# Large SBUF tiles handed out first in a fixed sequence, each beginning on a whole 128-byte line

## The chip, the cores and the metric

The kernel runs on one core of one Trainium2 chip. The metric is device time in microseconds of that core, the median of several runs. The core has five engines that run side by side: TensorE (PE, matrix products; its weight loads are listed as PEld), VectorE (DVE), ScalarE (ACT), GpSimd (POOL) and SyncE (SP), which here only issues DMA transfers. SBUF, the memory that the engines work in, has 128 partitions; a tile takes the same bytes in each of them, so that its place is one address within a partition.

## The reference

Two kinds of layer alternate, four in all, on a 2048 x 512 activation in float32. Layer A is a two-dimensional Fourier filter, layer B a gated bilinear feed-forward block with 1792 hidden features.

```python
def _A_ref(x, w_r, w_i):
    B, S, D = x.shape
    X = jnp.fft.rfft2(x, axes=(-2, -1))
    X = X * (w_r + 1j * w_i)
    return jnp.fft.irfft2(X, s=(S, D), axes=(-2, -1))

def _B_ref(x, w_gate, w_up, w_down):
    g = jnp.einsum("bsd,df->bsf", x, w_gate)
    u = jnp.einsum("bsd,df->bsf", x, w_up)
    return jnp.einsum("bsf,fd->bsd", g * u, w_down)

x = A_x
x = x + _A_ref(_layernorm(x), A_w_r, A_w_i)
x = x + _B_ref(_layernorm(x), B_w_gate, B_w_up, B_w_down)
x = x + _A_ref(_layernorm(x), A_w_r, A_w_i)
x = x + _B_ref(_layernorm(x), B_w_gate, B_w_up, B_w_down)
```

## The kernel before

**What it computes, and how.** The activation stays in SBUF throughout, as the tile `xs` of 16 blocks of 128 x 512. A Fourier layer is a chain of small float32 products (`fwd` with the tile `tp`, `middle` with `dp`, `zp` and `vq`, `inv` with `yi` and `yo`). A feed-forward layer splits every float32 factor into a high and a low part in the type float32r and takes three products in place of one: high by high, high by low, low by high (`mm3`). It also saves products of blocks by sums and differences of the blocks (the forms of the input in the tiles `xA` and `xS`, those of the weights in `wt`). One call of `prod` in `unit` is six matmuls of one weight form (stationary, a slice of 128 columns of `wt`) with one input form (moving, 512 or 256 columns of `xA` or `xS`); a call of `unit` is seven such products, named `gw, gx, gy, gx, gz, gv, gz` after the PSUM tile that they write. The way down again takes one of two paths: in the first half of the first layer, and at the very end of the second, `db` products (stationary the hidden block `h`, moving the weights `wd`, 512 columns); elsewhere `down`, with forms of hidden blocks as stationary operand (`sf`, or a part of a `bf` tile) and forms of the down weights as moving one (`bf`, 256 columns), into `ex, ey, ew, ez, ev`.

**What sets the order.** Every operation is recorded in `Plan` and then put out in the sequence that the table `ORDER` holds; a second table, `PLACES`, says which buffer of its ring a tile gets. The engines keep this order. Nothing in it is decided from addresses.

**What sets the addresses.** The three pools of SBUF and PSUM hand out addresses one after the other. A buffer is known by its tag (ring and number, such as `xA0` or `f3`) and gets its place when a tile of that tag is first asked for, that is when the first operation that uses it is put out (`Tile_.__call__` calls `make`, which calls `wk.tile`). Every buffer is rounded up to 32 bytes. The pool `cp` comes first and ends at byte 52,128 of a partition with the tile `hp`; the pool `wk`, with all other tiles of SBUF, begins there. So the offsets of the buffers of `wk` within a line of 128 bytes come from what small buffers (`st`, `mv`, `rs`: 32 bytes each) happened to be asked for before them. The built program has these places (bytes; in brackets the remainder by 128):

```text
buffer                             before            after
xs, midt, ident (pool cp)     16512.. [0]       the same
xA0: forms of the input       101792 [32]        52224 [0]
xS0: forms of the input        64928 [32]        76800 [0]
wa0, wa1, wb0, wb1: wt   196064, 202208,   109568, 123904,
                   218592, 210400 [96]   115712, 130048 [0]
rg0: slots of sf, raw weights  97696 [32]       138240 [0]
sx0: slots of sf, u            224736 [96]      142336 [0]
e0: E, xf, hw                  150784 [0]       146432 [0]
h0: bf, h, tws                  54176 [32]      179200 [0]
wd0: bf, wd, a part of wq      132000 [32]      187392 [0]
f0 to f10 (11 buffers of 2 KB)    all four       all four
dc, dj, tw (df, di, twiddles)         [32]            [0]
```

Whatever slice of 128 columns of a large tile a matmul takes, it lies a multiple of 512 bytes from the tile's beginning and so has the tile's remainder.

In this document two operands of a matmul have **equal offsets** when stationary and moving operand begin at the same remainder. Before, `db` products have equal offsets (`wd` and `h` at 32; both parts of `hw`, at the end, at 0). Products with `wt` do not (96 and 32). Products with `bf` do when the stationary operand is in `rg0` or in a `bf` tile (1,044 of 1,680 matmuls), and do not when it is in `sx0` (636).

All instructions of the plan carry the line of the helper that records them (L307 in the profile), so that the rows below are told apart by their tiles.

Of the kernel before, what the change touches and what calls it, by code (L numbers as in the profile page):

```python
# [11 lines left out]
F32 = mybir.dt.float32  # L12
# [90 lines left out]
SWAPS = "2212212212212212", "2212212212212212"  # L103
FAST = (0, 1)
IDLE = 2, 3
FAHEAD, BOFF, COFF, IOFF, W1, HPDUE, TOFF = 2.79, 9.0, 6.0, 5.0, 10.0, 40.0, 6.0
UFIRST = 5.0
UNITS = ((7.5, 17.4, 15.0), (7.2, 16.9, 16.9)), ((7.2, 16.9, 14.5), (7.2, 14.5, 14.5))
# [168 lines left out]
def kernel(ctx: ExitStack, tc: tile.TileContext, x, wf, wc, wb, dfwd, tf, ti, mid, out):  # L277
    nc = tc.nc
    cp = ctx.enter_context(tc.tile_pool(name="cp", bufs=1))
    wk = ctx.enter_context(tc.tile_pool(name="wk", bufs=1))  # L280
    pp = ctx.enter_context(tc.tile_pool(name="pp", bufs=1, space=bass.MemoryType.PSUM))
    dr = ctx.enter_context(tc.tile_pool(name="dr", bufs=1, space=bass.MemoryType.DRAM))
    plan = Plan()
# [49 lines left out]
    def load(kb, fn, r, w, **kw):  # L333
        return plan.op("SP", 0.1, 2.5, fn, r, w, kb=kb, **kw)
# [49 lines left out]
    def load_di():  # L384
        t = temp("di", "dj", (128, 4, 256))
        load(512, lambda: SP.dma_start(t(), dfwd[:, 512:1536].rearrange("p (b n) -> p b n", b=4)), (), [t])
        return t
# [123 lines left out]
    def keep_warm(n):  # L511
        for i in range(n):
            bk = bank("wp", "w")
            pe(0.86, lambda bk=bk: TE.matmul(bk(), midt[:, 0:128], midt, start=True, stop=True), ["midt"], [bk, "idle"])
# [462 lines left out]
    for layer in range(2):  # L977
        dcs["i"] = load_di()
        keep_warm(IDLE[layer])
        for g in range(16):  # L980
# [22 lines left out]
        t = t1  # L1003
# [21 lines left out]
        for k, (ft, half, h0) in enumerate(seq):  # L1025
# [32 lines left out]
            else:  # L1058
                first = ft // 2 not in blocks or (half is not None and (ft // 2, half) not in begun)
# [24 lines left out]
        else:  # L1084
            for t in range(8, 16):
                load(256, lambda t=t: SP.dma_start(out[:, t], xs[:, t]), [("xs", t)], [("out", t)], due=t0)
    for o in plan.order():
        o["fn"]()


# [42 lines left out]
```

## Time and profile before

| | us |
|---|---|
| median of 3 runs | 1082.05 (1081.18 to 1082.25) |
| the profiled execution | 1080.65 |
| its span, first to last instruction | 1078.9 |
| PE busy in it | 1054.7 |
| DVE, POOL, ACT busy | 817.1, 752.2, 406.5 |

What lies around the span is 1080.65 - 1078.9 = 1.75 us. The granted TensorE clock is 0.999 of full speed over the span.

How to read the rows: a row of a timeline gives the start of a run of instructions, the time from the start of the first to the end of the last, the tiles out<-in, the partitions by columns of the stationary operand, the shape of the output, and their number. Matmuls are pipelined: the next one starts long before the last has ended, so the pace is read from the starts of rows that follow each other, not from the duration of one. Six matmuls to a row is one product.

### The profile page before, as it was taken

To read this page: it belongs to the slowest core of one execution; us is meant where nothing else is said; L and a number is where in the kernel's file an instruction comes from. 1 tells how busy PE (TensorE), PEld (TensorE's weight loads), DVE (VectorE), ACT (ScalarE), POOL (GpSimd) and SP (SyncE) were. 2 spreads that over 40 slices of the span, in tenths; PEclk is the share of its full clock that TensorE was granted. 3 is DMA by queue.
4 is the path that set the end of the run, shared out by engine and by line. 5 is a ranking of instruction groups with operands and counts; after the bars stand their busy time and mean duration, and the time that the engine had idled before them with its cause. 6 is when DMAs were issued, how large, how long until landed. Compare 5 with 4: busy or idle time off the path is not lost.

```text
span 1078.9 us, 18673 instructions
## 1 busy us (share of the span) xinstructions
PE 1054.7 (98%) x6546; PEld 900.9 (84%) x6546; DVE 817.1 (76%) x1603; ACT 406.5 (38%) x965; POOL 752.2 (70%) x1000
## 2 busy tenths in 40 slices
PE   8999999999999999999989999999999999999998
PEld 6677888887899888889967779888788998888897
DVE  7677876668877567777897688688788876677688
ACT  6458534344344223223254484222323431222321
POOL 6847698989999666677747037455678994666772
PEclk9999999999999999999999999999999999999999
DMA  9514356778754765556390004465777255565542
GB/s 357 231 39 179 106 176 217 228 253 281 231 179 159 263 208 165 193 168 212 114 370 4 1 16 139 165 212 160 242 216 230 80 177 204 205 205 176 195 147 79
DMA packets 84668, 193.65 MB, mean 179 GB/s; under 512 B 39264, under 2 KB 50784, under 8 KB 73568
## 3 DMA queue, kind: packets, MB, share of 16 engines
q0 software_dynamic: 16128, 102.77, 28.8%
q1 hardware_dynamic: 68160, 89.18, 24.5%
q8 instruction: 52, 0.85, 0.3%
q10 hardware_dynamic: 288, 0.52, 0.1%
q14 instruction: 40, 0.33, 0.1%
HBM read 145.52 MB, written 46.92 MB: 178 GB/s over the span
## 4 chain that ended last, share of the span: by engine, by line
PE 80%; POOL 6%; DVE 5%; DMA 2%; issue 2%; ACT 2%; SPq 0%; DVEq 0%; POOLq 0%; ACTq 0%
PE gx L307 13%; PE gz L307 12%; PE gw L307 6%; PE gy L307 6%; PE gv L307 6%; PE db L307 5%; PE ex L307 5%; PE ez L307 4%; PE dp L307 3%; PE yi L307 3%; PE zp L307 3%; PE ev L307 2%; PE ew L307 2%; PE ey L307 2%; PE vq L307 2%; PE yo L307 2%
## 5 line engine op out<-in xcount | busy, mean ns | idle before, releaser
L307 PE MATMUL gx<-xA,wt 128*128 128x512 f32 (+1 forms) x852 | 181.5, 348 | 2.3 <-ACT s L307 2.3
L307 PEld LDWEIGHTS gx<-xA,wt 128*128 128x128 f32 x852 | 136.0, 188 | 21.9 <-ACT s L307 2.5
L307 DVE TENSOR_TENSOR xs<-xs,db 128x512 f32<-128x512 f32 x128 | 85.1, 679 | 21.6 <-PE db L307 21.2
L307 POOL TENSOR_TENSOR sf<-cc,sf 128x256 fp32r<-128x256 f32 x103 | 75.9, 740 | 24.7 <-ACT sf L307 24.3
L307 PE MATMUL gz<-xS,wt 128*128 128x512 f32 (+1 forms) x426 | 91.5, 350 | 1.1 <-DVE q L307 1.1
L307 PE MATMUL db<-wd,h 128*128 128x512 f32 x336 | 91.8, 397 | 0.0
L307 PE MATMUL gw<-xS,wt 128*128 128x512 f32 (+1 forms) x426 | 90.9, 348 | 0.3 <-POOL xS L307 0.2
L307 PE MATMUL gy<-xS,wt 128*128 128x512 f32 (+1 forms) x426 | 91.0, 349 | 0.0
L307 PE MATMUL gz<-xA,wt 128*128 128x512 f32 (+1 forms) x426 | 90.7, 348 | 0.0
L307 PE MATMUL gv<-xS,wt 128*128 128x512 f32 (+1 forms) x426 | 90.3, 347 | 0.0
L307 POOL TENSOR_TENSOR sf<-q,sf 128x256 fp32r<-128x256 f32 x89 | 65.6, 739 | 32.4 <-ACT sf L307 31.8
L307 PEld LDWEIGHTS gz<-xS,wt 128*128 128x128 f32 x426 | 68.6, 188 | 12.8 <-DVE q L307 1.7
L307 PEld LDWEIGHTS gw<-xS,wt 128*128 128x128 f32 x426 | 68.9, 188 | 11.5 <-POOL xS L307 0.7
L307 DVE TENSOR_TENSOR q<-gy,s 128x512 f32<-128x512 f32 (+1 forms) x71 | 40.9, 577 | 49.1 <-PE gy L307 26.5
L307 PEld LDWEIGHTS gy<-xS,wt 128*128 128x128 f32 x426 | 68.3, 188 | 10.4 <-issue 0.5
L307 PEld LDWEIGHTS gv<-xS,wt 128*128 128x128 f32 x426 | 68.2, 188 | 10.2 <-issue 0.7
L307 PEld LDWEIGHTS gz<-xA,wt 128*128 128x128 f32 x426 | 68.3, 188 | 10.1 <-issue 0.5
L307 ACT COPY s<-gx 128x512 f32<-128x512 f32 (+1 forms) x71 | 35.2, 496 | 105.0 <-PE gx L307 94.6
L307 POOL TENSOR_TENSOR wt<-rg,wt 128x512 fp32r<-128x512 f32 (+1 forms) x56 | 64.1, 1155 | 12.4 <-ACT wt L307 12.4
L307 PEld LDWEIGHTS db<-wd,h 128*128 128x128 f32 x336 | 61.0, 188 | 13.3 <-issue 1.2
L307 ACT CAST sf<-q 128x256 fp32r<-128x256 f32 x89 | 36.2, 406 | 87.2 <-DVE q L307 35.5
L307 POOL DMA_DIRECT2D wt<-gu x72 | 40.5, 563 | 35.5 <-PE gw L307 22.4
(163 smaller groups left out, 2551.3 us busy)
## 6 DMA issues: line engine op xcount, KB each, us to landing
wt<-gu POOLq DMA_DIRECT2D x36, 1024.0 KB, 5.3
wt<-gu POOLq DMA_DIRECT2D x36, 768.0 KB, 5.0
bf<-dn POOLq DMA_DIRECT2D x20, 1024.0 KB, 5.5
wq<-in_wf_dram SPq DMA_DIRECT2D x16, 1024.0 KB, 12.7
bf<-dn POOLq DMA_DIRECT2D x20, 768.0 KB, 4.7
gu<-wt SPq DMA_DIRECT2D x14, 1024.0 KB, 6.3
gu<-wt SPq DMA_DIRECT2D x14, 768.0 KB, 5.8
rg<-in_wb_dram SPq DMA_DIRECT2D x14, 512.0 KB, 4.3
```

What stands on the lines that cost most here:

```text
L307: ins = f(*args, **kw)
```

## The change

The change puts a table `PLACED` ahead of the placing of all buffers. It looks up the first tile of each tag in the order of the plan, then asks for these tiles in the table's sequence; an entry that is a number asks for a buffer of so many bytes per partition that nothing uses. The gap of 96 bytes takes the beginning of the pool from 52,128 to 52,224, a multiple of 128, and the sizes of the large tiles are all multiples of 128. After them the plan is put out as before, and the rest of the buffers get their places behind the large ones, in the order in which they are first used.

```diff
+PLACED = (96, 'xA0', 'xS0', 'wa00', 'wa10', 'wb00', 'wb10', 'rg0', 'sx0', 'e0', 'h0', 'wd0')
...
-    for o in plan.order():
+    order = plan.order()
+    first = {}
+    for o in order:
+        for t in o["tiles"]:
+            first.setdefault(t.tag(), t)
+    for n, p in enumerate(PLACED):
+        if isinstance(p, int):
+            wk.tile([128, p // 4], F32, name=f"gap{n}", tag=f"gap{n}", bufs=1)
+        else:
+            first[p]()
+    for o in order:
         o["fn"]()
```

On every engine the built program has the same instructions in the same order with the same waits; only addresses and the numbers in tile names differ. The DRAM tiles, the banks of PSUM and the tiles of `cp` keep their places.

## The prediction

> **What bounds the kernel now.** I read the page's busy times and chain first, then the busy times by stage, then TensorE's groups by shape, and last the timeline of PE, where the pace of matmuls stands.
>
> ```profile
> span 1078.9 us, 18673 instructions
> PE 1054.7 (98%) x6546; PEld 900.9 (84%) x6546; DVE 817.1 (76%) x1603; ACT 406.5 (38%) x965; POOL 752.2 (70%) x1000
> PE 80%; POOL 6%; DVE 5%; DMA 2%; issue 2%; ACT 2%; SPq 0%; DVEq 0%; POOLq 0%; ACTq 0%
> ```
>
> The stages, each with its length and then the busy time of PE, PEld, DVE, ACT and POOL in it:
>
> ```profile
> 130.00:300.00 170.00, 170.00 (x774) 137.96 (x773) 127.78 (x241) 63.68 (x125) 153.78 (x163) 1.00 0.71 230
> 300.00:345.00 45.00, 44.82 (x320) 41.60 (x319) 33.39 (x76) 21.05 (x51) 44.63 (x47) 1.00 0.49 178
> 825.00:890.00 65.00, 63.40 (x529) 62.48 (x529) 49.22 (x97) 24.89 (x59) 60.49 (x76) 1.00 0.44 149
> ```
>
> PE is busy for 98% of the span and is 80% of the chain that ended last. It leaves nothing idle between 130 and 300 us, and POOL is nearly full in two short stages (44.63 of 45 us). So a change that moves no instruction can move the time in one way above all: by the pace at which PE takes its matmuls. These are the large groups:
>
> ```profile
> L307 PE MATMUL gx<-xA,wt 128*128 128x512 f32 x492 | 128.7, 397 | 2.3 <-ACT s L307 2.3
> L307 PE MATMUL gv<-xS,wt 128*128 128x512 f32 x246 | 64.0, 395 | 0.0
> L307 PE MATMUL db<-wd,h 128*128 128x512 f32 x336 | 91.8, 397 | 0.0
> L307 PE MATMUL db<-hw 128*128 128x512 f32 x48 | 12.5, 396 | 0.0
> L307 PE MATMUL gx<-xA,wt 128*128 128x256 f32 x360 | 52.8, 282 | 0.0
> L307 PE MATMUL gv<-xS,wt 128*128 128x256 f32 x180 | 26.3, 282 | 0.0
> L307 PE MATMUL ex<-bf,sf 128*128 128x256 f32 x396 | 57.6, 282 | 0.3 <-DVE q L307 0.3
> L307 PE MATMUL ew<-bf 128*128 128x256 f32 x48 | 7.0, 281 | 0.0
> ```
>
> With `wt` there are 492 + 5 x 246 = 1,722 matmuls of 512 columns (`gx`, and five groups like the `gv` row) and 360 + 5 x 180 = 1,260 of 256; with `bf` 1,680 of 256 (the groups between the `ex` and `ew` rows), 1,044 of them at equal offsets and 636 not. 336 + 48 are `db`. These 5,046 are all in float32r.
>
> **The pace depends on the offsets.** 512 columns first:
>
> ```profile
> 273.82 1.56 PE L307 MATMUL gx<-xA,wt 128*128 128x512 f32 x6
> 275.22 1.56 PE L307 MATMUL gv<-xS,wt 128*128 128x512 f32 x6
> 276.62 1.56 PE L307 MATMUL gz<-xA,wt 128*128 128x512 f32 x6
> 278.02 1.55 PE L307 MATMUL db<-wd,h 128*128 128x512 f32 x6
> 279.40 1.56 PE L307 MATMUL gw<-xS,wt 128*128 128x512 f32 x6
> ```
>
> With `wt` (offsets 96 and 32) six matmuls take 1.40 us, 233.3 ns each. The six `db` behind them (both at 32) take 1.38 us, 230 ns. At the very end ten `db` from `hw`, both at 0 as all operands will be after the change, run undisturbed:
>
> ```profile
> 1071.22 2.43 PE L307 MATMUL db<-hw 128*128 128x512 f32 x10
> ```
>
> 2.43 us less the 0.39 us of one `db` (by its row, 396 ns) over nine steps is 226.7 ns. Six of the same kind a little earlier, between products of 256 columns, took 1.39 us, 231.7 ns:
>
> ```profile
> 1065.79 1.55 PE L307 MATMUL db<-hw 128*128 128x512 f32 x6
> 1067.18 0.86 PE L307 MATMUL gz<-xA,wt 128*128 128x256 f32 x6
> ```
>
> So equal offsets reach their pace only after some matmuls in which nothing interrupts; I call these settled. With 256 columns the order is the other way about:
>
> ```profile
> 516.23 0.84 PE L307 MATMUL gw<-xS,wt 128*128 128x256 f32 x6
> 516.91 0.88 PE L307 MATMUL ez<-bf 128*128 128x256 f32 x6
> 517.63 0.87 PE L307 MATMUL gz<-xS,wt 128*128 128x256 f32 x6
> 518.34 0.87 PE L307 MATMUL gv<-xS,wt 128*128 128x256 f32 x6
> ```
>
> With `wt` a product takes 0.68 us (516.91 - 516.23), 113.3 ns each, or 0.71 us, 118 ns (518.34 - 517.63): two paces of the same kind of operands, the slow one behind a product at equal offsets. That one, `ez<-bf` with both operands at 32, takes 0.72 us: 120 ns. The exchange of shapes matters too:
>
> ```profile
> 300.32 1.55 PE L307 MATMUL db<-wd,h 128*128 128x512 f32 x6
> 301.70 0.87 PE L307 MATMUL gz<-xS,wt 128*128 128x256 f32 x6
> ```
>
> ```profile
> 398.79 0.86 PE L307 MATMUL ew<-bf 128*128 128x256 f32 x6
> 399.49 1.05 PE L307 MATMUL tp<-tw,fo 128*128 128x128 f32 x8
> ```
>
> Behind 256 columns, six `db` at equal offsets take 1.38 us, 230 ns. Behind a product of 512 columns, `ew<-bf` at equal offsets takes 0.70 us, 117 ns. Equal offsets are thus worth some 7 ns to a settled matmul of 512 columns, and cost 2 to 7 ns to one of 256.
>
> **The change, part by part.** It makes every pair of large operands an equal pair, at 0. Before the sum, what it does not touch: the order of instructions, the waits and the transfers are the same on every engine and queue, so nothing is queued behind anything new; asking for a tile early costs no instruction.
>
> The other engines, and TensorE's float32 products. POOL's tiles lie at all four remainders now, and its rows show no difference: `sf` at 32 and 96 against `fo` out of `xs` at 0. The float32 products take two matmuls of half the pace each, and one with a moving operand at 32 (`tw`) is as long as one with it at 0 (`ident`).
>
> ```profile
> L307 POOL TENSOR_TENSOR sf<-cc,sf 128x256 fp32r<-128x256 f32 x103 | 75.9, 740 | 24.7 <-ACT sf L307 24.3
> L307 POOL TENSOR_TENSOR fo<-xs 128x256 f32<-128x256 f32 x38 | 26.9, 736 | 7.9 <-DMA xs<-in_x_dram 5.7 <-DVE gz L307 2.2
> L307 PE MATMUL tq<-ident,xn 128*128 128x128 f32 x64 | 9.6, 274 | 0.4 <-ACT sx L307 0.3
> L307 PE MATMUL tp<-tw,fo 128*128 128x128 f32 x64 | 8.4, 274 | 0.0
> L307 PE MATMUL ev<-bf,sf 128*128 128x256 f32 x186 | 27.1, 281 | 0.8 <-DMA bf<-dn 0.8
> ```
>
> I take 0 for both. Transfers from and to the moved tiles may become a little shorter or longer; PE's groups waited 0.8 us for a transfer (the `ev` row), which bounds this term at 0.8 us to either side. I take 0 here too: the transfers are hidden by the matmuls around them, and what they cost without that cover is those 0.8 us.
>
> The matmuls of 512 columns with `wt`. Between 130 and 300 us there are 120 + 5 x 60 = 420 of them, with `db` in between and little else:
>
> ```profile
> L307 PE MATMUL db<-wd,h 128*128 128x512 f32 x246 | 66.5, 397 | 0.0
> L307 PE MATMUL gx<-xA,wt 128*128 128x512 f32 x120 | 31.3, 396 | 0.0
> L307 PE MATMUL gv<-xS,wt 128*128 128x512 f32 x60 | 15.6, 395 | 0.0
> ```
>
> After the change nothing unsettles them there but a few `yo` and `yi`. I take 227 ns: 420 x (233.3 - 227) = 2.6 us less. The 246 `db` of this stage, now at about 230.5, settle too: 246 x 3.5 = 0.9 us less. The other 1,302 stand in runs of six to eighteen between products of 256 columns. The first six behind 256 columns need 230 ns at equal offsets, those behind them 226.7. I take 229.5: 1,302 x 3.8 = 4.9 us less. Bounds for all 1,722: 11.4 us less (226.7 everywhere) and nothing.
>
> The matmuls of 256 columns. With `wt` they now run at 113.3 to 118, taken as 116.5; at equal offsets 120 when settled and 117 behind 512 columns, taken as 119: 1,260 x 2.5 = 3.2 us more. With `bf`, the 636 at unequal offsets from about 116 to 118.5: 1.6 us more; the 1,044 at equal offsets stay, but for those that settle only now, 0.3 ns on average: 0.3 us more. Bounds: all 2,940 at 120, which is 1,260 x 3.5 + 636 x 4 + 1,044 x 1.3 = 8.3 us more; or all at 113.3, which is 1,260 x 3.2 + 636 x 2.7 + 1,044 x 5.4 = 11.4 us less.
>
> The sum is -2.6 - 0.9 - 4.9 + 3.2 + 1.6 + 0.3 = -3.3 us. All of it lies on PE's path where PE has no idle time; between 130 and 300 us POOL is busy for 153.78 of 170 us, so that it can follow a PE that is 3.5 us quicker there. In the two stages that POOL fills, the slower 256 columns leave POOL some room, which could give back a few tenths; I count none. Against the profiled execution: 1080.65 - 3.3 = 1077.35 us (span 1075.6). That execution lies 1.4 us below the median of the runs, so against the median: 1082.05 - 3.3 = 1078.75.
>
> A rule speaks against all of this. The Trainium skill, TensorE: Matmul & The Clock Gate, "Step-by-step: what each phase is for", has two independent SBUF read ports, one for the moving operand and one for the weight load, so that loading the next weights takes nothing from the running matmul; and SBUF — State Buffer, "Specifications (TRN2)", has lines of 16 bytes, of which 32 and 96 are whole multiples already. By these rules offsets are worth nothing, and the sum would be 0. The trace does not agree for this type: the same shape runs at 113.3, 118 and 120 ns, and 120 goes with equal offsets.
>
> **The rivals.**
>
> *The beginning itself counts.* An operand at 0 may be read in fewer pieces than one at 32, and then 256 columns get the short pace with equal offsets too. No row shows 256 columns at 0, which speaks for leaving it open; against it, `hw` at 0 takes 1.39 us for its six at 1065.79 and `wd,h` at 32 1.38 us at 278.02, as if only the difference of the two offsets counted. Time: 11.4 (512 with `wt`) + 1.2 (336 `db` x 3.5) + 11.4 (256) = 24 us less, 1058; halfway, 1070.
>
> *The pace follows from what ran before, not from the offsets.* The two paces of the same operands with `wt` speak for it; that `ez<-bf` and `db` differ from their neighbours each time speaks against. Time: 1082, within 1 us.
>
> *Slower: equal offsets never settle at 512 columns.* Place: the runs of six to eighteen, and the exchange of `xA` and `xS` and of the `wt` tiles at every product; the settled rows are from ten matmuls on one pair of tiles at the end of the program, with nothing behind them. If 512 columns stay at 230.5, they give 1,722 x 2.8 = 4.8 us and `db` nothing, and if 256 columns settle at 120 everywhere, they cost 8.3: 3.5 us more, 1085.6. With 256 columns at 120 the change breaks even when 512 columns reach 233.3 - 8.3 us / 1,722 = 228.5 ns; above that it is slower.
>
> **How the numbers follow.** The forecast has a chance of 0.42 and a range of its own of 1074 to 1082; the beginning itself 0.18 (1058 to 1072); no effect 0.15; slower 0.25 (1083 to 1090). The time is that of the forecast, 1078.8. The range for 8 in 10 leaves out the far half of the second case and the far end of the last: 1062 to 1087. About 0.2%, 2.2 us, is what a measurement of this kernel tells from no change. Faster by more: 0.36 of the forecast's 0.42, all 0.18 and 0.02 of the third case, 0.56. Within 0.2%: 0.05 + 0.11 + 0.03 = 0.19. Slower: 0.01 + 0.02 + 0.22 = 0.25.
>
> **What would show it.** In the changed profile: the starts of products with `wt` of 512 columns between 130 and 300 us 1.36 us apart (now 1.40); products of 256 columns of all kinds 0.70 to 0.72 us apart, and none at 0.68; the end of the stage that now ends at 300 us some 3 us earlier, and the stages of 256 columns about 1 us longer in all; POOL's and DVE's means unchanged. Products of 256 columns at 0.68 throughout would show the first rival, rows that are as before the second, 1.38 or more for 512 columns the third. A new wait of PE on POOL between 130 and 300 us would prove the cover wrong that I counted on there.

## The result and the profile after

The changed kernel takes 1079.29 us, the median of 20 runs (1076.78 to 1082.75), against 1081.43 us (1079.75 to 1083.44, 20 runs) of the kernel before beside it: a ratio of 0.9979, with an interval of 0.9969 to 0.9989. It is faster by 0.21%, about 2.1 us. The profiled execution took 1077.16 us.

The head of its page:

```profile
span 1075.4 us, 18673 instructions
PE 1052.6 (98%) x6546; PEld 907.4 (84%) x6546; DVE 817.4 (76%) x1603; ACT 406.0 (38%) x965; POOL 753.4 (70%) x1000
```

PE is as busy a share as before, and DVE and POOL do the same work in the same time (817.1 and 752.2 us before). The same stages by busy time (PE, PEld, DVE, ACT, POOL), at the same places of the span:

```profile
130.00:300.00 170.00, 169.87 (x792) 140.47 (x791) 128.93 (x243) 64.00 (x127) 155.85 (x164) 1.00 0.71 235
300.00:345.00 45.00, 45.00 (x320) 42.29 (x320) 33.76 (x78) 20.86 (x51) 44.56 (x49) 1.00 0.45 163
825.00:890.00 65.00, 64.78 (x525) 63.70 (x525) 50.40 (x99) 24.32 (x58) 57.60 (x72) 1.00 0.43 141
```

Between 130 and 300 us PE fits 792 matmuls where it fitted 774. POOL is busy for 155.85 us instead of 153.78 and follows. PE's 0.18 us of idle time in the next stage is gone, and between 825 and 890 us it is busy for 64.78 us instead of 63.40. The large groups by shape:

```profile
L308 PE MATMUL gx<-xA,wt 128*128 128x512 f32 x492 | 127.0, 393 | 1.9 <-ACT s L308 1.9
L308 PE MATMUL db<-wd,h 128*128 128x512 f32 x336 | 91.0, 395 | 0.1
L308 PE MATMUL gx<-xA,wt 128*128 128x256 f32 x360 | 53.8, 285 | 0.0
L308 PE MATMUL ex<-bf,sf 128*128 128x256 f32 x396 | 58.4, 284 | 0.1
L308 PE MATMUL ev<-bf,sf 128*128 128x256 f32 x186 | 27.4, 283 | 0.0
L308 POOL TENSOR_TENSOR sf<-cc,sf 128x256 fp32r<-128x256 f32 x103 | 76.1, 742 | 23.5 <-ACT sf L308 22.0 <-PE ew L308 1.1
```

Products of 512 columns became shorter (397 to 393 ns with `wt`), those of 256 longer (282 to 285 with `wt`, 282 to 284 with `bf`). POOL's mean is unchanged (740 and 742 ns). PE's wait of 0.8 us for the transfer `bf<-dn`, which stood in the `ev` row, is gone. The paces themselves stand in the timeline of PE, first in the stage from 130 to 300 us:

```profile
273.18 1.52 PE L308 MATMUL gv<-xS,wt 128*128 128x512 f32 x6
274.54 1.52 PE L308 MATMUL gz<-xA,wt 128*128 128x512 f32 x6
275.90 1.52 PE L308 MATMUL db<-wd,h 128*128 128x512 f32 x6
277.26 1.52 PE L308 MATMUL gw<-xS,wt 128*128 128x512 f32 x6
```

All starts are 1.36 us apart, 226.7 ns a matmul, where products with `wt` were 1.40 apart and `db` 1.38. And in a stage that mixes both shapes:

```profile
443.84 1.52 PE L308 MATMUL gy<-xS,wt 128*128 128x512 f32 x6
445.20 0.88 PE L308 MATMUL ez<-bf,sf 128*128 128x256 f32 x6
445.92 1.55 PE L308 MATMUL gx<-xA,wt 128*128 128x512 f32 x6
447.30 1.52 PE L308 MATMUL gz<-xS,wt 128*128 128x512 f32 x6
448.66 0.88 PE L308 MATMUL ez<-bf 128*128 128x256 f32 x6
```

A product of 256 columns takes 0.72 us, 120 ns each. The product of 512 columns right behind it takes 1.38 us (447.30 - 445.92, 230 ns), and the next one 1.36 (448.66 - 447.30).

To compare whole kernels I take the mean distance from the start of one matmul to the start of the next over all matmuls of a class, leaving out those with an interruption in between. By this measure, before and after:

| class, number | before, ns | after, ns | change, us |
|---|---|---|---|
| 512 columns with `wt`, 1,722 | 233.18 | 229.01 | -7.2 |
| 512 columns, `db`, 383 | 231.43 | 229.14 | -0.9 |
| 256 columns with `wt`, 1,260 | 116.40 | 119.64 | +4.1 |
| 256 columns with `bf`, 1,680 | 117.66 | 119.34 | +2.8 |
| sum | | | -1.2 |

The paces are thus worth 1.2 us. The two profiled spans differ by 3.5 us and the medians by 2.1; the rest of the 3.5 is time in which PE waits.

### The profile page after: what moved, and what is told of

It reads as the page before. It is cut to its first block, busy times and chain, and to the rows that moved or that the text cites. A ratio compares the mean times of both kernels' runs of the same rounds, so it can differ in the third digit from the quotient of the medians.

```text
span 1075.4 us, 18673 instructions
## 1 busy us (share of the span) xinstructions
PE 1052.6 (98%) x6546; PEld 907.4 (84%) x6546; DVE 817.4 (76%) x1603; ACT 406.0 (38%) x965; POOL 753.4 (70%) x1000
## 4 chain that ended last, share of the span: by engine, by line
PE 82%; DVE 5%; POOL 3%; issue 2%; ACT 2%; DMA 2%; SPq 0%; DVEq 0%; POOLq 0%; ACTq 0%
PE gx L308 13%; PE gz L308 13%; PE gw L308 7%; PE gv L308 6%; PE gy L308 6%; PE db L308 6%; PE ex L308 5%; PE ez L308 5%; PE dp L308 3%; PE zp L308 3%; PE yi L308 3%; PE ew L308 2%; PE ey L308 2%; PE ev L308 2%; PE vq L308 2%; PE yo L308 2%
```

## The experiments

All kernels are the changed one with another table `PLACED`, so that instructions, order and waits are again the same and only addresses differ. The differences and paces of all of them are in one table at the end of this section; "difference" is the beginning of the stationary tile less that of the moving one, with whole multiples of 512 bytes left out.

### Does the beginning itself count, or the place in the pool?

All large tiles together at 32 in place of 0, and the tiles in the reverse order:

```diff
-PLACED = (96, 'xA0', 'xS0', 'wa00', 'wa10', 'wb00', 'wb10', 'rg0', 'sx0', 'e0', 'h0', 'wd0')
+PLACED = (128, 'xA0', 'xS0', 'wa00', 'wa10', 'wb00', 'wb10', 'rg0', 'sx0', 'e0', 'h0', 'wd0')
```

> The large tiles in the order of the change, but all at remainder 32 by 128 (a gap of 128 bytes in place of 96). Theory (only the difference of the two operands' offsets counts): as the change, ratio to before 0.998 (0.996 to 1.000); with wt 227 ns per matmul of 512 columns between 130 and 300 us and 229.5 elsewhere, 119.5 ns per matmul of 256 columns. Rival (the beginning on a whole line counts): 512 columns back at 233 ns, 256 columns at 120, ratio 1.002 to 1.007.

```diff
-PLACED = (96, 'xA0', 'xS0', 'wa00', 'wa10', 'wb00', 'wb10', 'rg0', 'sx0', 'e0', 'h0', 'wd0')
+PLACED = (96, 'wd0', 'h0', 'e0', 'sx0', 'rg0', 'wb10', 'wb00', 'wa10', 'wa00', 'xS0', 'xA0')
```

> The change with the sequence of the large tiles turned round, all at remainder 0 at other addresses. Theory (remainders alone): the paces of the change, ratio to before 0.998 (0.996 to 1.000). Rival (the place in SBUF or the distance of the tiles counts): other paces, ratio off by more than 0.002 from the change's.

Measured: 1079.91 us with all at 32, ratio 0.9983 (0.9972 to 0.9994), and 1078.68 us turned round, ratio 0.9970 (0.9958 to 0.9983). Both have the paces of the change to 0.2 ns in every class. The timeline of PE with all at 32:

```profile
445.72 1.52 PE L308 MATMUL gy<-xS,wt 128*128 128x512 f32 x6
447.08 0.88 PE L308 MATMUL ez<-bf,sf 128*128 128x256 f32 x6
447.80 1.55 PE L308 MATMUL gx<-xA,wt 128*128 128x512 f32 x6
449.18 1.52 PE L308 MATMUL gz<-xS,wt 128*128 128x512 f32 x6
```

1.36, 0.72, 1.38: these are the steps of the changed kernel, with no large tile on a whole line. Neither the beginning of a tile nor its place in the pool counts; the difference between tiles is left.

### One difference of 64 bytes at a time

First `wt` alone at 64 from `xA` and `xS`, then the slots of `sf` alone at 64 from `bf` (64 bytes before it). Every other pair of operands keeps its difference of 0, but in both kernels `h`, `wd` and `bf`, and in the first `sf` too, come to lie 128 bytes off `xA` and `xS`:

```diff
-PLACED = (96, 'xA0', 'xS0', 'wa00', 'wa10', 'wb00', 'wb10', 'rg0', 'sx0', 'e0', 'h0', 'wd0')
+PLACED = (96, 'xA0', 'xS0', 64, 'wa00', 'wa10', 'wb00', 'wb10', 64, 'rg0', 'sx0', 'e0', 'h0', 'wd0')
```

> The change with the four wt tiles alone moved to remainder 64. Theory: products with wt go back to the pace of before, 233 ns at 512 columns (1,722 x 4.2 = 7.2 us more) and 116.5 at 256 (1,260 x 3.2 = 4.1 us less), bf products stay at 119.3; 3.1 us slower than the change, ratio to before 1.001 (0.999 to 1.003). Rival (the beginning of the moving tile counts, xA and xS stay at 0): ratio 0.996 to 0.999, 512 columns below 230 ns.

```diff
-PLACED = (96, 'xA0', 'xS0', 'wa00', 'wa10', 'wb00', 'wb10', 'rg0', 'sx0', 'e0', 'h0', 'wd0')
+PLACED = (96, 'xA0', 'xS0', 'wa00', 'wa10', 'wb00', 'wb10', 64, 'rg0', 'sx0', 64, 'e0', 'h0', 'wd0')
```

> The change, but the two buffers that hold sf (rg0, sx0) at remainder 64, all others at 0. Theory: the 1,338 matmuls of 256 columns that read sf fall back from 119.3 ns to 116 (113.3 or 118 each), 512 columns keep 227 and 229.5 ns, wt with 256 columns keeps 119.6; 1,338 x 3.3 = 4.4 us quicker than the change if all of it reaches the end, half of it if waits take the rest: ratio to before 0.994 to 0.996. Rival (the beginning counts): sf off the line costs, ratio 0.999 to 1.003.

Measured: `wt` at 64 gives 1083.48 us, ratio 1.0007 (0.9994 to 1.0020). The products with `wt` go back to 232.1 ns at 512 columns and 115.6 at 256, those with `bf` stay at 119.1. `sf` at 64 gives 1076.68 us, ratio 0.9952 (0.9938 to 0.9966), and beats both kernels. Its timeline, over the products shown of the change:

```profile
444.03 1.53 PE L308 MATMUL gy<-xS,wt 128*128 128x512 f32 x6
445.40 0.87 PE L308 MATMUL ez<-bf,sf 128*128 128x256 f32 x6
446.11 1.52 PE L308 MATMUL gx<-xA,wt 128*128 128x512 f32 x6
447.47 1.53 PE L308 MATMUL gz<-xS,wt 128*128 128x512 f32 x6
448.83 0.88 PE L308 MATMUL ez<-bf 128*128 128x256 f32 x6
449.55 1.55 PE L308 MATMUL gv<-xS,wt 128*128 128x512 f32 x6
450.93 0.87 PE L308 MATMUL ex<-bf,sf 128*128 128x256 f32 x6
```

The product with `sf` takes 0.71 us, and the 512 columns behind it 1.36, at once at the short pace. Behind `ez<-bf`, both operands of which come from `bf` tiles and are still equal, they take 1.38. So the change gave each class the same difference, though the two shapes want different ones: 512 columns are quickest with equal offsets, and 256, of the two differences tried so far, with 64.

### The gap alone, and the change once more

```diff
-PLACED = (96, 'xA0', 'xS0', 'wa00', 'wa10', 'wb00', 'wb10', 'rg0', 'sx0', 'e0', 'h0', 'wd0')
+PLACED = (96,)
```

> Only the gap of 96 bytes stays; no tile is asked for early. The differences between the operands are those of before (64 bytes with wt and sx0, none with rg0, bf and db), while every tile's own remainder has moved on by 96. Theory: the paces of before, 233.2 ns (512 columns with wt), 231.4 (db), 116.4 (256 with wt), 116.1 and 118.6 (256 with bf), PE's wait for bf<-dn at 513 us of 0.6 to 0.8 us is back, ratio 1.000 within 0.0015. Rival (the tiles' own beginnings, or the start of the pool on a whole line, made part of the gain): ratio 0.998 to 0.999 with the paces of before, and no wait for bf<-dn.

And the change as it is, beside the others of its set:

> The changed kernel once more, beside the three others of this set. Theory (the paces are a property of the offsets): 512 columns with wt at 229.0 ns on average and 227 between 130 and 300 us, 256 columns at 119.6 with wt and 119.3 with bf, as in the first profile of it; PE does not wait for bf<-dn at 513 us; ratio 0.998, between 0.996 and 0.999. Rival (the transfer's length, 6.74 us before and 5.40 us after, is a matter of one execution): the paces repeat, but PE waits for bf<-dn again by some 0.8 us and the span is that much longer than the 1075.4 us of the first profile.

Measured: the gap alone 1081.06 us, ratio 0.9991 (0.9979 to 1.0002), with the paces of before to 0.1 ns and PE's wait for `bf<-dn` (0.5 us) back. The change once more: 1079.35 us, ratio 0.9980 (0.9965 to 0.9995), its paces those of the first profile to 0.1 ns, and no wait for `bf<-dn` at 513 us. Yet its span was 1077.5 us, not 1075.4. PE's waits between 770 and 860 us in the first profile of the change, with the idle time and its releaser at the end:

```profile
777.90 1.66 PE L308 MATMUL gx<-xA,wt 128*128 128x512 f32 x6 [1.90 <-ACT s L308]
...
824.76 0.98 PE L308 MATMUL gz<-xS,wt 128*128 128x256 f32 x6 [1.13 <-DVE q L308]
...
835.50 0.74 PE L308 MATMUL ez<-bf,sf 128*128 128x256 f32 x4 [0.16 <-POOL sf L308]
```

The same in the second profile of the same program:

```profile
778.80 1.66 PE L308 MATMUL gx<-xA,wt 128*128 128x512 f32 x6 [2.40 <-ACT s L308]
...
825.46 0.98 PE L308 MATMUL gz<-xS,wt 128*128 128x256 f32 x6 [0.93 <-DVE q L308]
...
833.94 0.74 PE L308 MATMUL ev<-bf,sf 128*128 128x256 f32 x4 [0.40 <-POOL sf L308]
...
837.42 0.74 PE L308 MATMUL ez<-bf,sf 128*128 128x256 f32 x4 [0.35 <-POOL sf L308]
...
852.32 0.95 PE L308 MATMUL ex<-bf,sf 128*128 128x256 f32 x6 [0.23 <-DMA bf<-dn]
```

These add up to 3.19 us in the one and 4.31 in the other: 1.1 of the 2.1 us between the spans, with no address changed. With the shorter stops that the rows leave out, the second profile falls 1.7 us behind in this stretch, by the starts of the same products. Between 300 and 500 us, where PE waits for nothing, the two executions stay 0.17 us apart throughout. So paces can be compared between two profiles to a tenth of a nanosecond, while two spans differ by 2 us for the waits alone. Of the 3.5 us between the first two spans the medians confirm 2.1.

### Differences of 32 and 96, and whole lines apart

```diff
-PLACED = (96, 'xA0', 'xS0', 'wa00', 'wa10', 'wb00', 'wb10', 'rg0', 'sx0', 'e0', 'h0', 'wd0')
+PLACED = (96, 'xA0', 'xS0', 32, 'wa00', 'wa10', 64, 'wb00', 'wb10', 64, 'rg0', 64, 'sx0', 32, 'e0', 'h0', 'wd0')
```

> Differences of 32 and of 96 bytes, which no kernel so far has: xA, xS, h0 and wd0 at 0, half of the wt tiles at 32 and half at 96, the slots of sf at 32 (rg0) and 96 (sx0). Theory (equal or not is all that counts): both halves of wt pace as at 64, 232 to 233 ns at 512 columns and 115.6 to 116.4 at 256, sf with bf 117 to 117.5; ratio 1.0000, between 0.998 and 1.002. First rival (the difference counts in steps): the two halves differ by more than 1 ns at 512 columns or at 256, one nearer to the equal pace of 229 and 119.6. Second rival (lines of 64 bytes, of which 32 and 96 are the same half): both halves have one pace, but another than at 64, say 231 and 118.

```diff
-PLACED = (96, 'xA0', 'xS0', 'wa00', 'wa10', 'wb00', 'wb10', 'rg0', 'sx0', 'e0', 'h0', 'wd0')
+PLACED = (96, 'xA0', 'xS0', 128, 'wa00', 'wa10', 'wb00', 'wb10', 'rg0', 'sx0', 256, 'e0', 'h0', 'wd0')
```

> The remainders by 128 are all 0 as in the change, but the wt tiles lie 128 bytes further on (remainder 128 by 512) than xA and xS, and sf 256 bytes from bf. So far all kernels with equal offsets had them equal by 512 as well. Theory (a line of 128 bytes): the paces of the changed kernel, 229.0 ns (512 columns with wt), 119.6 (256 with wt), 119.3 (256 with bf); ratio 0.998, between 0.996 and 0.999. Rival (a line of 256 or 512 bytes): wt at 232 to 233 ns and 115.6 to 116.4 as with a difference of 64; by a line of 512 sf with bf at 117.3 as well; ratio 0.999 to 1.001.

Measured with 32 and 96: 1082.47 us, ratio 1.0009 (0.9998 to 1.0019). At 512 columns the two halves of `wt` pace at 233.1 (32) and 233.6 ns (96), as at 64. At 256 columns they take 118.3 and 117.9, more than the 115.6 to 116.4 at 64, so the theory of equal or not was too simple there, by 2 ns. The products with `sf`, expected at 117 to 117.5, took 119.3 from `rg0` and 117.3 from `sx0`. By 256 bytes these slots lie 96 and 32 before `bf` (by 128: 32 and 96 behind it), and at 96 before it they are no quicker than at 0.

The kernel with lines apart surprised me. Every large tile begins on a whole 128-byte line from every other, as in the change, and it took 1083.34 us, ratio 1.0013 (1.0001 to 1.0024), with `wt` of 512 columns at 232.4 ns. My theory of a line of 128 bytes predicted 229.0. Three differences had been moved at once, though, so two kernels with `wt` alone moved followed.

### 128 or 256 bytes

```diff
-PLACED = (96, 'xA0', 'xS0', 'wa00', 'wa10', 'wb00', 'wb10', 'rg0', 'sx0', 'e0', 'h0', 'wd0')
+PLACED = (96, 'xA0', 'xS0', 'rg0', 'sx0', 'e0', 'h0', 'wd0', 128, 'wa00', 'wa10', 'wb00', 'wb10')
```

> All large tiles at remainder 0 by 512, but the wt tiles 128 bytes further on; so one difference alone, of 128 bytes, and nothing of sf, h or wd is moved against anything as in the kernel with lines apart. First theory (offsets count by more than 128 bytes): 512 columns with wt at 231.5 to 233 ns everywhere, also between 130 and 300 us, 256 with wt at 118 to 119; no gain, ratio 0.9995 to 1.002. Rival (a line of 128 bytes does count, and what slowed the kernel with lines apart were sf, h and wd): the paces of the changed kernel, 227 ns between 130 and 300 us and 229.0 in all, ratio 0.998.

The other has 256 in the place of 128.

> The same with 256 bytes. Theory that offsets count by 512 bytes: 512 columns with wt at 231 to 233 ns, 256 at 118 to 119, ratio 0.9995 to 1.002. Rival (they count by 256 bytes): the paces of the changed kernel, 227 ns between 130 and 300 us, 229.0 in all, 119.6 at 256 columns; ratio 0.998.

Measured: 1083.03 us with 128, ratio 1.0007 (0.9995 to 1.0019), and 1080.02 us with 256, ratio 0.9980 (0.9967 to 0.9993). The timelines of PE over the products shown of the change, with 128 first:

```profile
274.01 1.56 PE L308 MATMUL gx<-xA,wt 128*128 128x512 f32 x6
275.40 1.56 PE L308 MATMUL gv<-xS,wt 128*128 128x512 f32 x6
276.80 1.56 PE L308 MATMUL gz<-xA,wt 128*128 128x512 f32 x6
278.20 1.53 PE L308 MATMUL db<-wd,h 128*128 128x512 f32 x6
279.57 1.56 PE L308 MATMUL gw<-xS,wt 128*128 128x512 f32 x6
```

Products with `wt` are 1.39 to 1.40 us apart, as before the change, and `db`, whose own operands are still equal, 1.37. With 256:

```profile
274.24 1.52 PE L308 MATMUL gv<-xS,wt 128*128 128x512 f32 x6
275.60 1.52 PE L308 MATMUL gz<-xA,wt 128*128 128x512 f32 x6
276.96 1.52 PE L308 MATMUL db<-wd,h 128*128 128x512 f32 x6
278.32 1.52 PE L308 MATMUL gw<-xS,wt 128*128 128x512 f32 x6
```

1.36 everywhere, and all four classes within 0.3 ns of the change. So for 512 columns 128 bytes are as unequal as 64 (231.9 and 232.1 ns), and 256 as equal as 0: their pace goes by the difference by 256 bytes. For 256 columns a difference of 128 (119.1 ns) is hardly told from 0 (119.6); there the rival named for the kernel with lines apart, 115.6 to 116.4, missed. The change makes all large tiles equal by 256 too, since it puts each of them on a multiple of 512.

### The best placement

`sf` at 64 once more, and then with `sf` placed last, so that `h` and `wd` stay equal by 256 to the other tiles (with `sf` in the middle they lie 128 bytes off `xA`, `xS` and `wt`):

> The kernel with sf at 64 once more, since its ratio of 0.9952 came from five runs. Theory (256 columns with sf at 117.3 and 512 with wt at 228.3 ns are worth 1,338 x 2.0 + 1,722 x 0.7 = 3.9 us to the changed kernel, of which some is given back as waits): ratio 0.995 to 0.997. Rival (those five runs were short by chance): 0.998 as the changed kernel.

```diff
-PLACED = (96, 'xA0', 'xS0', 'wa00', 'wa10', 'wb00', 'wb10', 'rg0', 'sx0', 'e0', 'h0', 'wd0')
+PLACED = (96, 'xA0', 'xS0', 'wa00', 'wa10', 'wb00', 'wb10', 'e0', 'h0', 'wd0', 64, 'rg0', 'sx0')
```

> sf at 64 as in that kernel, but placed last, so that h and wd stay at 0 by 512 (there they lay 128 bytes off xA, xS and wt, and the stage from 130 to 300 us ran at 228.6 ns with wt and 229.5 for db, against 227.0 and 227.8 in the changed kernel). Theory (offsets of all operands that follow each other count, by 512): 227.0 and 227.8 between 130 and 300 us, 228.2 in the mixed stages, 117.3 for sf; 420 x 1.6 + 250 x 1.7 = 1.1 us less than with sf at 64, ratio 0.994 to 0.996. Rival (sf's new distance to the other tiles is what slowed that stage): 228.6 there again, and the time of the kernel with sf at 64 within 0.5 us.

Measured: `sf` at 64 again 1076.92 us, ratio 0.9948 (0.9928 to 0.9968), so its gain is no chance. `sf` last: 1078.09 us, ratio 0.9952 (0.9932 to 0.9971). The stage from 130 to 300 us settled as expected (227.1 ns with `wt`, 227.7 for `db`, against 228.6 and 229.4). But the 512 columns of the mixed stages did not keep their 228.2: they are at 229.7, as in the change. That half of the theory fell. Between the two kernels two things differ: where `bf` lies against `xA` and `xS` (128 bytes off, and 0), and on which side of `bf` the slots of `sf` lie (64 before it, and 64 behind). Either may be what lets 512 columns reach the short pace behind a product of 256; no run moves one alone. The ratios of the two overlap; which is better is open.

| kernel | `wt` from `xA`, `xS` | `sf` from `bf` | ratio | 512 with `wt` | `db` | 256 with `wt` | 256 with `bf` |
|---|---|---|---|---|---|---|---|
| before | 64 | 0 (rg0), 64 (sx0) | 1 | 233.2 | 231.4 | 116.4 | 117.7 |
| gap alone | 64 | 0 (rg0), 64 (sx0) | 0.9991 | 233.2 | 231.5 | 116.3 | 117.7 |
| the change | 0 | 0 | 0.9979 | 229.0 | 229.1 | 119.6 | 119.3 |
| all at 32 | 0 | 0 | 0.9983 | 229.0 | 229.2 | 119.6 | 119.4 |
| turned round | 0 | 0 | 0.9970 | 229.0 | 229.3 | 119.7 | 119.3 |
| `wt` at 256 | 256 | 0 | 0.9980 | 229.0 | 229.4 | 119.6 | 119.3 |
| `wt` at 128 | 128 | 0 | 1.0007 | 231.9 | 230.6 | 119.1 | 119.0 |
| lines apart | 128 | 256 | 1.0013 | 232.4 | 230.7 | 119.0 | 118.7 |
| 32 and 96 | 32, 96 | -96 (rg0), -32 (sx0) | 1.0009 | 233.3 | 230.3 | 118.1 | 118.4 |
| `wt` at 64 | 64 | 0 | 1.0007 | 232.1 | 230.2 | 115.6 | 119.1 |
| `sf` at 64 | 0 | -64 | 0.9952 | 228.3 | 230.5 | 119.3 | 117.8 |
| `sf` last, at 64 | 0 | 64 | 0.9952 | 229.0 | 229.3 | 119.6 | 117.9 |

Differences are by 512 bytes, with a minus where the stationary tile lies before the moving one; paces are in ns, by the measure of the first section.

## Why the prediction was right, and where it was off

The forecast was a kernel quicker by 3.3 us, 1078.8 us against the median; 1079.29 was measured. The mechanism was the one forecast. Step by step:

- **512 columns with `wt` between 130 and 300 us**: 233.2 to 227 was predicted, 227.04 measured, 2.6 us both times. The starts 1.36 us apart are those that the text asked for. The product that began at 300.32 us before begins at 297.84, 2.5 us earlier, where some 3 were asked for.
- **`db` of that stage**: 230.96 to 227.78, 0.8 us; predicted 0.9.
- **The other 1,302**: 229.5 predicted, 229.6 to 229.7 in the three mixed stages, 4.6 us instead of 4.9. The working was right in detail too: six at 230 behind 256 columns, 226.7 for those after them.
- **256 columns**: this term was mis-sized. With `wt` I took 119 ns and got 119.64 (+4.1 us, not +3.2). The 636 unequal ones with `bf` went from 116.1 to 119.3 (+2.1, not +1.6), the 1,044 equal ones from 118.6 to 119.3 (+0.8, not +0.3). I had allowed for products right behind 512 columns at 117; in the changed kernel they take 120 there as well, as `ez<-bf,sf` at 445.20 shows. The loss is 6.9 us where the sum had 5.1.
- **The sum of the paces** is thus -1.2 us, not -3.3, and the median moved by 2.1. Counted from each matmul to the next, paces put both profiles of the change 1.3 us ahead of the one before, and waits put the first 2.2 us ahead and the second 0.1. The sum took the waits as zero, so that 1078.8 lies this near to 1079.29 partly by luck.
- **The wait for `bf<-dn` at 513 us**, 0.8 us before, is gone in both profiles of the change, but not by its paces. In all fourteen profiles PE is ready for the transfer 5.96 to 6.18 us after its issue. What differs is the transfer. It takes 6.34 to 6.74 us in the seven profiles with a wait of 0.3 us or more (before, the gap alone, `wt` at 64, 32 and 96, `wt` at 256, `sf` at 64 once, `sf` last), and 5.36 to 6.09 in the seven others. Kernels with equal offsets of `wt` are in both groups. The one program with `sf` at 64 has 6.46 us and a wait in one execution:

```profile
511.20 0.92 PE L308 MATMUL ev<-bf,sf 128*128 128x256 f32 x6 [0.46 <-DVE cc L308]
```

and 5.63 us and none in the other:

```profile
509.57 0.87 PE L308 MATMUL ev<-bf,sf 128*128 128x256 f32 x6
```

The first row names DVE, but PE starts 0.13 us after the transfer has landed, as it does in the other six (0.13 to 0.14). So the rival of the repeated run is borne out in this much: the transfer's length varies from one execution to the next. Whether the placement has any part in it these runs don't show. The 0.8 us are within the bound that the prediction set for transfers.

- **The other engines**: POOL's rows as before. PE has a new wait between 130 and 300 us, of 0.1 us in the `db` row and 0.3 in the second profile, but on DVE, not on POOL, and the stage kept its gain: the cover held.
- **"The beginning itself counts"** fell: at 32 the paces are the same. **"What ran before, no effect"** fell: `wt` at 128 and at 256 differ in one number, and the 512 columns by 231.9 and 229.0 ns. What ran before does matter for the size: `db`, equal in all kernels, runs at 229.1 to 231.5 ns by its neighbours' offsets. **"Slower"** came nearer than its wording: the break-even stood at 228.5 ns for 512 columns with all 256 columns at 120; measured were 229.0 and 119.5, and by paces alone 1.2 us were left.

The time was right, yet one definition under it was too narrow. I took equal offsets to be equal by 128 bytes, which is also what the change says of itself. The runs with 128 and 256 show that for 512 columns they must be equal by 256. It did no harm only because the differences before (64) are unequal by either measure and those after (0) equal by either.

The Trainium skill's rule of two independent read ports (TensorE: Matmul & The Clock Gate, "Step-by-step: what each phase is for"), by which loading weights takes nothing from the running matmul, stays at odds with these runs for float32r. Where the weights lie should then not matter, yet moving them alone by 128 bytes changes the pace of 512 columns by 2.9 ns. What couples the two no run shows.

## What to carry to other kernels

Where PE is the bound and an instruction count can't fall, compare the starts of like matmuls by the offsets of their operands, and do it for each shape apart: one common alignment helped 512 columns by 4.2 ns and cost 256 columns 1.7 to 3.2. Place the operands by pair and shape rather than all on one line, with differences taken by 256 bytes: `wt` equal and `sf` at 64 gave 0.9952 and 0.9948, more than twice the gain of the change. For 256 columns try the difference: 64 made them quicker on either side, while 128, and 96 before, gave next to nothing. And judge such a change by paces, not by two spans, which differ by 2 us for the same program.

## What the runs showed of the hardware that I had not expected

**256 bytes.** The pace of float32r matmuls of 512 columns depends on the difference of the operands' addresses by 256 bytes: 228.3 to 229.0 ns with a difference of 0 or 256, and 231.9 to 233.6 with 32, 64, 96 or 128. What in the chip makes 256 the step no run here shows.

**The clock, for 3.4 us at a time.** In seven of the fourteen profiles the granted clock falls to 0.50 for 3.4 us in the midst of the program, behind waits of PE: near 80 us in four (all at 32, turned round, `wt` at 256, the gap alone), and near 778 us in all three with `sf` at 64. The stretch with all at 32, whose first 0.5 us lie ahead of the fall, and then the same one of the change (columns as in the stages above; the third from the end is the clock):

```profile
79.50:82.00 2.50, 2.50 (x7) 2.03 (x8) 0.00 (x0) 0.70 (x2) 1.95 (x2) 0.60 0.00 0
```

```profile
79.50:82.00 2.50, 2.50 (x13) 2.22 (x12) 0.00 (x0) 1.18 (x4) 2.21 (x3) 1.00 0.00 0
```

At 0.60 PE started 7 matmuls where it started 13. Each of the four lost 1.7 us there; at 778 us the three lost some 1.5. This is `sf` at 64, first the stretch with the wait and then the fall:

```profile
774.40:777.80 3.40, 0.99 (x9) 0.75 (x7) 0.40 (x2) 0.66 (x2) 0.57 (x1) 1.00 1.01 270
777.80:781.20 3.40, 3.40 (x10) 2.84 (x11) 3.40 (x7) 0.91 (x3) 0.00 (x0) 0.51 0.53 171
```

The traces show no need of the placement for it. In each of them the clock changes only at whole steps of 3.41 us after it first stands at 1.00, which is 4.2 to 6.9 us into the span. Near 76 and 79 us PE waits 1.31 and 0.68 us in all fourteen. In the four with a fall there, PE is idle for 1.70 to 1.95 us of one step and the next step is the slow one; in the ten others no step there has more than 1.45 us. Near 778 us it is 2.2 to 2.4 us in the three, and at most 1.76 in the others. So the fall goes with the wait and with where the steps happen to lie in an execution. The figures of the two places overlap (1.76 without a fall, 1.70 with one), so that no bound can be read from them.

The timed runs go with their clock as well: of the 32 runs of the change, the 11 at 0.999 or 1.000 have a median span of 1075.9 us and the 21 at less have 1078.6. Two times of one program thus differ by the clock too, and not by waits alone.
